# Twelve V loads cut by partitions, and a reordered turn, in an attention and MLP decode step with its gradients

## The chip, the cores and the metric

The kernel runs on one core of a Trainium2 chip. The metric is the device time of one execution in microseconds (us). A core has engines that run side by side: PE (matrix products; PEld is its weight load), DVE (vector operations), ACT (scalar functions and scaling), POOL and SP. In this kernel POOL only issues stores and SP only issues loads. The transfers themselves are done by 16 DMA engines, which all queues share. Each DMA engine that takes part in a transfer adds 1 to the transfer's semaphore when its part has landed, so that a transfer of 128 rows ends with 16 increments.

## The reference

One token x (1 x 640) goes through a block with attention over a cache of 8192 positions (32 heads of 192) and an MLP of width 1536, with layer norms modulated by a vector c. The function returns the output and, for a given grad_out, the gradients of nine inputs, those of the whole K and V cache among them. Cut to what fills the time:

```python
q = (x @ wq).reshape(B, Sq, Hq, Dh)                      # after layer norm and modulation
scores = einsum('bhqd,bhkd->bhqk', q, k) * Dh ** -0.5
p = softmax(scores)
o = einsum('bhqk,bhkd->bhqd', p, v);  ao = o @ wo
x1 = x + ga * ao                                         # then layer norms, MLP: gelu(n @ w3) @ w4
# gradients, per head: do is the gradient of o
# dV[k, :] = p[k] * do          dP[k] = sum_d V[k, d] * do[d]
# dS[k] = p[k] * (dP[k] - c)    dK[k, :] = dS[k] * q
```

K and V are 100.7 MB each, and so are dK and dV. V is read twice, once forward and once backward; K is read once.

## The kernel before, in words

**Layout.** The 8192 positions of a head lie as 64 rows on each of 128 partitions. Everything is done in halves: half t (0 or 1) of head h is a tile of 128 partitions x 32 rows x 192 values in bf16, that is 12288 bytes per partition and 1536 KB in all. In the diff "rows" of a load are partitions. `load_k` (L234) and `load_v` (L328) load such a half in one transfer, issued on SP.

**Forward (L592 to L659).** Step i of the loop works on three heads: it makes the scores of head i, scales K of head i-1 by its softmax weights, and ends the sums of head i-2. Scores: DVE multiplies a K half by q (`fwd_mult`, "prod" at L132), PE sums the products over d by matrix products with an identity (L372), DVE reduces them (L376), and after a maximum (L383 to L391) ACT takes the exponential (L393). ACT (L407) and DVE (L414) scale K rows by the weights into EK, and PE forms the products of V with EK (L432, L443, L449), from which both the forward output and, later, the gradient of q are made. In each second step a small sum (`fwd_tot`, L476) waits on PE until DVE has added up the part of ao (`fwd_ao_add`, L618), and DVE does that behind its second prod of the step. Loads are issued on SP in program order, per step V half 0, in each second step a wo tile (`fwd_wo`, L460), K half 1 of the next head, V half 1, K half 0 of the head after. Each waits for its buffer: three for V, five "big" ones for K.

**Turn (L660 to L1230).** After the last head comes a chain of small operations: the end of ao, two layer norms (`ln_cols`), w3 and a gelu, then back (du, dn2, two `ln_bwd_cols` named lb2 and lb1) to the gradient of ao, from which the first do is made (L1201 to L1207). Beside this chain, other work is put where an engine would wait: `dg_some(n)` does n of the 12 products d_g = w4 rows with dbo on DVE (0.82 us each, L546); `w3T_pe` and `w3T_act` transpose w3 on PE (L699) through PSUM banks and copy it out on ACT (L704); `woT_some(n)` transposes n of four groups of a wo tile in the same way (L712, L713). The argument `fill` of the layer norms says what is put into which wait. The first dV store is issued at the end of the turn, at 570.9 us.

**Backward (L1231 on).** Heads run from 31 down. Per head DVE and ACT make the two dV halves (L983, L1005), DVE multiplies the loaded V halves by do (`bwd_mult`, "V_sb" at L132), PE sums them to dP (L1000), DVE makes dS and the two dK halves (L983). POOL issues the stores of dV (L1008), dK (L1035) and of the smaller gradients. V halves come through a ring of six buffers (`ring_load`, L749), which now and then also takes a wo tile (`load_wo`); SP loads the next one when the buffer's last use is over. The stores' tiles come from the five big buffers.

The order of work on PE, DVE and ACT is that of the program (`pin_order`, L53). Loads on SP use eight semaphores in turn, so a load also waits until the load eight places ahead of it has landed.

Of the kernel before, what the change touches and what calls it, by code (L numbers as in the profile page):

```python
# [20 lines left out]
def kernel(  # L21
# [26 lines left out]
    nc = tc.nc  # L48
# [16 lines left out]
    P = 128  # L65
# [6 lines left out]
    JH = J // 2  # L72
# [10 lines left out]
    NP2 = DH // 2  # L83
    NA = 8
    NAV = 40
    assert S % P == 0 and D % P == 0 and QD % P == 0 and F % P == 0 and DH == 192

    const = ctx.enter_context(tc.tile_pool(name="const", bufs=1))
# [5 lines left out]
    def bank(tag, bufs=1, name=None, n=512):  # L94
        return psum[0].tile([P, n], FP32, tag=tag, name=name or "ps_" + tag, bufs=bufs)
# [32 lines left out]
    def ccol(n, name, dtype=FP32):  # L128
        return const.tile([P, n], dtype, name=name)

    def mul(out, a, b):
        nc.vector.tensor_tensor(out=out, in0=a, in1=b, op=ALU.mult)  # L132

    def add(out, a, b):
        nc.vector.tensor_tensor(out=out, in0=a, in1=b, op=ALU.add)
# [4 lines left out]
    def stt(out, in0, scalar, in1, op0, op1):  # L140
        nc.vector.scalar_tensor_tensor(out=out, in0=in0, scalar=scalar, in1=in1, op0=op0, op1=op1)  # L141
# [6 lines left out]
    def neg_means(parts, n, name):  # L148
        ps = bank_c(name)
        nc.tensor.matmul(ps[:, 0:n], lhsT=negd_mat, rhs=parts, start=True, stop=True)  # L150
        return ps[:, 0:n]
# [21 lines left out]
    def ln_bwd_cols(dn, n, rstd, add_to, out, pfx, fill=lambda: None):  # L173
        s = ccol(2, pfx + "_s")
        nc.vector.reduce_sum(out=s[:, 0:1], in_=dn, axis=AX.X)
        jk = ccol(NDC, pfx + "_jk")
        nc.vector.tensor_tensor_reduce(out=jk, in0=dn, in1=n, scale=1.0, scalar=0.0, op0=ALU.mult, op1=ALU.add, accum_out=s[:, 1:2])
        m_ps = neg_means(s, 2, pfx + "_m")
        fill()
        t = ccol(NDC, pfx + "_t")  # L180
        mul(t, n, m_ps[:, 1:2].to_broadcast([P, NDC]))
        add(t, t, dn)
        add(t, t, m_ps[:, 0:1].to_broadcast([P, NDC]))
        stt(out, t, rstd[:, 0:1], add_to, ALU.mult, ALU.add)
# [23 lines left out]
    V_hd = [A_v_cache[0, h].rearrange("(p j) d -> p j d", p=P) for h in range(HQ)]  # L208
# [25 lines left out]
    def load_k(h, t):  # L234
        tl = big_tile("K_sb")
        nc.sync.dma_start(out=tl, in_=K_hd[h][:, t * JH : (t + 1) * JH, :])
        return tl
# [30 lines left out]
    x0_c, c_c, dy_c = xcg[:, 0:NDC], xcg[:, NDC : 2 * NDC], xcg[:, 2 * NDC : 3 * NDC]  # L268
# [56 lines left out]
            return (0, P), (P, DH), 0, 3 * (h // 2), 3 * (h // 2) + 1  # L325
        return (DH - P, DH), (0, DH - P), DH - P, 3 * (h // 2) + 2, 3 * (h // 2) + 1

    def load_v(pool, h, t, slot):  # L328
        tl = pool.tile([P, JH, DH], BF16, name="V_sb", tag=f"v{slot}")
        nc.sync.dma_start(out=tl, in_=V_hd[h][:, t * JH : (t + 1) * JH, :])  # L330
        return tl

    def load_fwd(h, t, kind):
        if not 0 <= h < HQ:
            return
        if kind == "v":
            st[h]["V"].append(load_v(fv, h, t, (2 * h + t) % 3))
        elif (h, t) not in K_st:
            K_st[h, t] = load_k(h, t)

# [181 lines left out]
    def fwd_ao_add(hp, sm, c1=408):  # L522
        if hp == 0:
            dve_copy(ao_c, sm[:, c1 : c1 + NDC])
        else:
            add(ao_c, ao_c, sm[:, c1 : c1 + NDC])
# [4 lines left out]
    def w3n(i, lo, hi):  # L531
        return w_t[1][:, i * F + lo : i * F + hi] if i < 4 else w_t[0][:, lo:hi]

    def w4n(f, lo, hi):
        return w_t[0][:, F + f * D + lo : F + f * D + hi] if f < 7 else w_t[2][:, (f - 7) * D + lo : (f - 7) * D + hi]
# [3 lines left out]
    def dg_some(n):  # L539
        f0 = dg_next[0]  # L540
        f1 = min(f0 + n, NFC)
        dg_next[0] = f1
        for f in range(f0, f1):
            j0 = 5 * D + 12 * P + f % 2 * D
            jk = w_t[2][:, j0 : j0 + D]
            nc.vector.tensor_tensor_reduce(out=jk, in0=w4n(f, 0, D), in1=dbo_bc, scale=1.0, scalar=0.0, op0=ALU.mult, op1=ALU.add, accum_out=d_g[:, f : f + 1])  # L546

    st = {h: {"V": [], "prod": []} for h in range(HQ)}
# [21 lines left out]
    fv = ctx.enter_context(tc.tile_pool(name="fv", bufs=1, side="right", reuse_waits="tile"))  # L570
# [21 lines left out]
    for i in range(1, HQ):  # L592
        c, p, pp = 2 <= i < HQ, 0 <= i - 1 < HQ, 0 <= i - 2 < HQ
        n = i + 1 < HQ
# [84 lines left out]
    def w3T(blk, n=1):  # L679
        if blk < NB3:  # L680
            return w3T_t[:, blk * P : (blk + n) * P]
        c0 = 5 * D + (blk - NB3) * P
        return w_t[2][:, c0 : c0 + n * P]

    w3T_next = [0, 0]
    w3T_ps = {}
    NG3 = NFC * NDC // 4

    def w3T_pe(n):
        for g in range(w3T_next[0], min(w3T_next[0] + n, NG3)):  # L690
            b = g % 6
            if b in (0, 2):
                w3T_ps[g] = bank("s", 2, "t_ps", SB[0])
                w3T_ps[g + 1] = w3T_ps[g][:, 512:1024]
            elif b > 3:
                w3T_ps[g] = bank("ab"[b - 4], name="t_ps")
            for k in range(4):
                f, i = divmod(4 * g + k, NDC)
                nc.tensor.matmul(w3T_ps[g][:, k * P : (k + 1) * P], lhsT=w3n(i, f * P, (f + 1) * P), rhs=ident_bf, start=True, stop=True)  # L699
        w3T_next[0] += n  # L700

    def w3T_act(n):
        for g in range(w3T_next[1], min(w3T_next[1] + n, NG3)):
            nc.scalar.copy(out=w3T(4 * g, 4), in_=w3T_ps[g][:, 0:512])  # L704
        w3T_next[1] += n

    def woT_some(n):
        for g in range(woT_next[0], min(woT_next[0] + n, 4)):
            t_ps = bank("s", 2, "t_ps", SB[0])
            blks = range(4 * g, min(4 * g + 4, 3 * NDC))  # L710
            for k, blk in enumerate(blks):
                nc.tensor.matmul(t_ps[:, k * P : (k + 1) * P], lhsT=woT[:, blk * P : (blk + 1) * P], rhs=ident_bf, start=True, stop=True)  # L712
            nc.scalar.copy(out=woT[:, 512 * g : 512 * g + P * len(blks)], in_=t_ps[:, 0 : P * len(blks)])  # L713
        woT_next[0] += n
# [4 lines left out]
    fwd_kvK(hl - 1, 3, st[hl - 1])  # L719
    nc.scalar.copy(out=kb_sb, in_=kb_ps[:, 0 : 2 * DH])  # L720
    fwd_ao_add(HH - 2, sl_["sm"])
    dg_some(1)
    fwd_ao_add(HH - 1, sl_["sm"], 420)
    fek_cm.__exit__(None, None, None)
    fsm_cm.__exit__(None, None, None)
# [7 lines left out]
    HS = list(range(HQ - 1, -1, -1))  # L733
    PS = list(range(HH - 1, -1, -1))
    V_b = {HS[0]: st[HS[0]]["V"], HS[1]: {1: st[HS[1]]["V"][1]}}
# [10 lines left out]
    def ring_slot(n):  # L746
        return (3, 4, 5, 2, 0, 1)[n % NR]

    def ring_load():  # L749
        while ring_n[0] < len(ring) and (ring_n[0] < 3 or ring_key(ring_n[0] - NR) in freed):  # L750
            kind, k, t = ring[ring_n[0]]
            slot = ring_slot(ring_n[0])
            pool = bv if slot > 2 else fv
            ring_n[0] += 1
            if kind == "v":
                V_b.setdefault(k, {})[t] = load_v(pool, k, t, slot)
            else:
                load_wo(k, pool.tile([P, JH, DH], BF16, name="V_sb", tag=f"v{slot}"))

    def load_wo(k, tl):  # L760
        lo, n = PS[BATCHES[k][-1]], len(BATCHES[k])
        tl = tl.rearrange("p j d -> p (j d)")[:, 0 : 3 * n * D].rearrange("p (c r) -> p c r", r=D)
        nc.sync.dma_start(out=tl, in_=wo_v[:, 3 * lo : 3 * (lo + n), :])
        for hp in range(lo, lo + n):
            for cc in range(3):
                wo_src[hp, cc] = tl[:, 3 * (hp - lo) + cc, :]

    def ring_key(n):
        return ring[n] if n >= 0 else (("v", HS[0], 0), ("v", HS[0], 1), ("v", HS[1], 1))[n]
# [9 lines left out]
    def bwd_pf_act(h):  # L779
        bst[h]["PF"] = bsm.tile([P, J], FP32, name="PF")  # L780
        nc.scalar.activation(out=bst[h]["PF"], in_=E_all[:, h, :], func=ACT.Copy, scale=rinv_bc[:, h : h + 1])
# [7 lines left out]
        bwd_pf_dve(h)  # L789

    def ln1_fill(k):
        if k == 0:
            dg_some(1)
        else:
            w3T_pe(4)
            w3T_act(4)

    def ln2_fill(k):
        w3T_pe(1 + 2 * k)
        dg_some(1)  # L800

    x1_c = ccol(NDC, "x1_c")
    mul(x1_c, ao_c, ga)
# [1 line left out]
    n1_c, r1 = ln_cols(x1_c, "ln1", ln1_fill)  # L805
# [48 lines left out]
    for f in range(NFC):  # L854
        for i in range(NDC):
            nc.tensor.matmul(dn2_ps[:, i : i + 1], lhsT=w3T(f * NDC + i), rhs=du_bf[:, f : f + 1], start=False, stop=(f == NFC - 1), skip_group_check=True)
    bwd_pf_act(HS[0])
    dn2 = ccol(NDC, "dn2")
    dve_copy(dn2, dn2_ps[:, 0:NDC])
    mid_ps = {"h2": aux_ps[:, 32 : 32 + NDC]}  # L860
# [4 lines left out]
                nc.tensor.matmul(mid_ps["h2"][:, r : r + 1], lhsT=w4n(f, r * P, (r + 1) * P), rhs=g_bf[:, f : f + 1], start=False, stop=(f == 6), skip_group_check=True)  # L865

    def lb2_fill():
        woT_some(4)

    dhb = ccol(NDC, "dhb")  # L870
    ln_bwd_cols(dn2, n2_c, r2, dbo_c, dhb, "lb2", lb2_fill)
    dn1 = ccol(NDC, "dn1")
    mul(dn1, dhb, cb1)
    dx1 = ccol(NDC, "dx1")
    ln_bwd_cols(dn1, n1_c, r1, dy_c, dx1, "lb1")
    dao_bf = ccol(NDC, "dao_bf", BF16)
    mul(dao_bf, dx1, ga)
    bwd_pf_dve(HS[0])
# [123 lines left out]

    def bwd_dv_act(o, h, t, lo=0, hi=NAV // 2):
        for jj in range(lo, hi):
# [4 lines left out]

    def bwd_dv_dve(o, h, t, na=NAV // 2, ends=(JH,)):  # L1010
        j0 = t * JH
# [219 lines left out]
    for i in range(HQ):  # L1231
        h, nxt = HS[i], HS[i + 1] if i + 1 < HQ else None
# [48 lines left out]
        if i == I_SIDE:  # L1281
# [5 lines left out]
            for n in range(len(ring) - NR, len(ring)):  # L1287
                slot = ring_slot(n)
# [33 lines left out]
```

## Time and profile before

| what | value |
|---|---|
| time, median of 3 runs (lowest to highest) | 1380.68 us (1379.69 to 1381.73) |
| profiled execution, its own time | 1382.5 us |
| its span, from the first to the last instruction | 1380.7 us |
| busy share of the span: PE, DVE, ACT, POOL | 62%, 78%, 68%, 8% |
| read from and written to HBM | 341.51 MB, 225.91 MB |
| V half: transfers, KB, median from issue to landing | 125, 1536 KB, 14.2 us |
| K half | 64, 1536 KB, 14.4 us |
| dK half, store | 64, 1536 KB, 23.0 us |
| dV half, store | 61, 1536 KB, 22.4 us |
| ACT before dV products (L1005), waiting for dK stores | 60.6 us |
| DVE before dK products (L983), waiting for dK stores | 54.0 us |

The page divides the span into 40 equal slices of 34.5 us; the forward takes the first 15 or so, the turn two, the backward the rest. A digit in the slices is a busy share in tenths. Lines of a timeline give start, duration, engine, line, operation, tiles and, in brackets, how long the engine was idle before and what ended that. Lines of windows give the stretch, its length, the busy time and count of instructions of PE, PEld, DVE, ACT and POOL, then the granted PE clock (1.00 is full), the share of the 16 DMA engines' time that was busy, and GB/s. The trace also holds the start, length, queue and size of each DMA packet and the time of each semaphore increment; it does not say which DMA engine made them.

### The profile page before, as it was taken

What the parts mean: (1) busy time and instruction counts of PE and PEld (TensorE: products, weight loads), DVE (VectorE), ACT (ScalarE), POOL (GpSimd) and SP (SyncE); (2) the same over time, 40 slices, a digit from 0 to 9 for tenths busy, and PEclk for the clock granted to TensorE, in tenths of its full rate; (3) what the DMA queues carried; (4) which work ended last, traced back from release to release, by engine and by line L of the source; (5) the groups of instructions that cost most, each with busy time, mean ns of one, the idle gap of its engine ahead of it and who ended that gap; (6) DMA issues with size and microseconds to landing.
All of it is one profiled execution on the core that took longest, in us unless ns stands there. A gap on an engine that the chain in (4) does not pass through costs nothing. (4 is left out here: it accounts for less than half of the span.)

```text
span 1380.7 us, 28348 instructions
## 1 busy us (share of the span) xinstructions
PE 852.1 (62%) x11655; PEld 672.8 (49%) x11655; DVE 1070.6 (78%) x1273; ACT 945.0 (68%) x2586; POOL 112.0 (8%) x203
## 2 busy tenths in 40 slices
PE   3699999999999999738645744234332435324242
PEld 3577777777777777726534532123221323213131
DVE  3588778878887886799997977857757859579695
ACT  1388777877877884866786657576864866557781
POOL 0000000000000000111101101111111111021010
PEclk9799999999999998566666666666766666666665
DMA  9999999999999999899999999999999999999997
GB/s 392 416 415 420 419 418 420 421 411 418 418 419 407 418 417 376 311 381 422 409 425 427 427 426 428 428 426 427 420 423 421 407 427 426 429 423 406 429 428 311
DMA packets 73167, 569.25 MB, mean 412 GB/s; under 512 B 6862, under 2 KB 19918, under 8 KB 32846
## 3 DMA queue, kind: packets, MB, share of 16 engines
q1 hardware_dynamic: 48592, 341.52, 60.2%
q0 software_dynamic: 24416, 225.92, 38.9%
q8 instruction: 91, 1.49, 0.4%
q14 instruction: 38, 0.31, 0.1%
q10 hardware_dynamic: 30, 0.00, 0.0%
HBM read 341.51 MB, written 225.91 MB: 411 GB/s over the span
## 5 line engine op out<-in xcount | busy, mean ns | idle before, releaser
L1005 ACT ACTIVATE dV<-do_pb,PF 128x192 bf16<-128x192 bf16 x1246 | 434.6, 440 | 108.7 <-DMA out_dram<-dK 60.6
L1000 PE MATMUL dP_ps<-V_sb,ident_bf 128*128 128x256 bf16 (+1 forms) x1584 | 229.2, 319 | 246.8 <-DVE V_sb L132 246.8
L407 ACT ACTIVATE EK<-K_sb,E_f 128x192 bf16<-128x192 bf16 x992 | 351.1, 442 | 4.1 <-PE kb_ps L302 2.8
L1000 PEld LDWEIGHTS <-ident_bf 128*128 128x128 bf16 x1584 | 179.3, 116 | 296.3 <-issue 169.1
L983 DVE TENSOR_TENSOR dK<-dS,q_pb 128x6144 bf16<-128x6144 bf16 x64 | 213.2, 3354 | 59.4 <-DMA out_dram<-dK 54.0
L132 DVE TENSOR_TENSOR prod<-K_sb,q_pb 128x6144 bf16<-128x6144 bf16 x64 | 214.4, 3349 | 3.6 <-DMA K_sb<-in_A_k_cache_dram 3.6
L132 DVE TENSOR_TENSOR V_sb<-V_sb,do_pb 128x6144 bf16<-128x6144 bf16 (+1 forms) x66 | 212.0, 3253 | 0.0
L432 PE MATMUL ps_a<-EK,V_sb 128*128 128x193 bf16 x1984 | 192.9, 249 | 1.9 <-DMA V_sb<-in_A_v_cache_dram 1.9
L432 PEld LDWEIGHTS <-V_sb 128*128 128x128 bf16 x1984 | 165.6, 99 | 19.5 <-issue 12.7
L983 DVE TENSOR_TENSOR dV<-P2h,do_pb 128x2304 bf16<-128x2304 bf16 (+2 forms) x67 | 88.8, 1353 | 50.1 <-DMA out_dram<-dV 40.4
L414 DVE TENSOR_TENSOR EK<-K_sb,P2h 128x1536 bf16<-128x1536 bf16 x124 | 117.5, 949 | 0.0
L1008 POOL DMA_DIRECT2D out_dram<-dV x68 | 37.0, 545 | 934.9 <-DVE dV L983 607.7
L443 PE MATMUL ps_b<-EK,V_sb 128*64 128x193 bf16 x1984 | 109.3, 253 | 0.0
L372 PE MATMUL S_ps<-prod,ident_bf 64*64 64x256 bf16 x3072 | 101.7, 280 | 11.9 <-DVE prod L132 11.9
L372 PEld LDWEIGHTS <-ident_bf 64*64 64x64 bf16 x3072 | 86.7, 111 | 32.6 <-issue 28.3
L443 PEld LDWEIGHTS <-V_sb 128*64 128x64 bf16 x1984 | 81.9, 110 | 19.7 <-issue 16.1
L393 ACT ACTIVATE E_f<-sm_ps,negm 128x64 f32<-128x64 f32 x31 | 9.7, 314 | 104.4 <-DVE negm L391 104.4
L376 DVE TENSOR_REDUCE S<-S_ps 128x128 f32<-128x1024 f32 x32 | 39.2, 1224 | 49.0 <-PE S_ps L372 49.0
L449 PE MATMUL kb_ps<-EK,hot_bf 128*32 128x384 bf16 x992 | 64.8, 339 | 0.0
L1050 ACT ACTIVATE wq_o<-wq_bc,ha_f 128x1536 bf16<-128x1536 bf16 x12 | 18.4, 1564 | 44.4 <-DMA out_dram<-wq_o 44.4
L191 PE MATMUL bc_ps<-ident_bf,dq_bf 128*128 128x128 bf16 x48 | 6.4, 304 | 66.6 <-ACT do_pb L195 65.5
L1035 POOL DMA_DIRECT2D out_dram<-dK x64 | 35.3, 552 | 136.7 <-DVE dK L983 95.1
(266 smaller groups left out, 805.8 us busy)
## 6 DMA issues: line engine op xcount, KB each, us to landing
V_sb<-in_A_v_cache_dram SPq DMA_DIRECT2D x125, 1536.0 KB, 14.2
K_sb<-in_A_k_cache_dram SPq DMA_DIRECT2D x64, 1536.0 KB, 14.4
out_dram<-dK POOLq DMA_DIRECT2D x64, 1536.0 KB, 23.0
out_dram<-dV POOLq DMA_DIRECT2D x61, 1536.0 KB, 22.4
wq<-in_A_wq_dram SPq DMA_DIRECT2D x3, 2560.0 KB, 33.9
wo_t<-in_A_wo_dram SPq DMA_DIRECT2D x16, 480.0 KB, 14.9
out_dram<-dwo POOLq DMA_DIRECT2D x16, 480.0 KB, 18.2
wq<-in_A_wq_dram SPq DMA_DIRECT2D x4, 1920.0 KB, 28.3
```

What stands on the lines that cost most here:

```text
L132: nc.vector.tensor_tensor(out=out, in0=a, in1=b, op=ALU.mult)
L372: nc.tensor.matmul(st["S_ps"][c0 : c0 + 64, r, t * JH : (t + 1) * JH, :], lhsT=ident_bf[64 * r : 64 * r + 64, 64 * r : 64 * r + 64], rhs=p ...
L376: nc.vector.reduce_sum(out=st["S2"], in_=st["S_ps"], axis=AX.X)
L407: nc.scalar.activation(out=st["EK"][q][:, jj, 0:DH], in_=K_st[h, t][:, r * JQ + jj, :], func=ACT.Copy, scale=st["E_f"][:, j : j + 1])
L414: nc.vector.tensor_tensor(out=EK[:, NA:JQ, 0:DH].rearrange("p j (d r) -> p j d r", r=2), in0=K_st[h, t][:, r * JQ + NA : (r + 1) * JQ, :]. ...
L432: nc.tensor.matmul(st["A_ps"][:, 0:n], lhsT=V_sb[:, r * JQ + jj, a0:a1], rhs=EK[:, jj, 0:n], start=(q == 0 and jj == 0), stop=(q == 3 and ...
L443: nc.tensor.matmul(st["B_ps"][g : g + 64, 0:n], lhsT=V_sb[:, r * JQ + jj, b0:b1], rhs=EK[:, jj, 0:n], start=(q == 0 and jj < 2), stop=(q = ...
L449: nc.tensor.matmul(kb_ps[g : g + 32, 0 : 2 * DH], lhsT=hot_bf[:, HQ - 1 - h : 2 * HQ - 1 - h], rhs=EK[:, jj : jj + 2, 0:DH], start=(h == 0 ...
L983: nc.vector.tensor_tensor(out=o.rearrange("p j (d r) -> p j d r", r=2), in0=pairs[:, :, None, :].to_broadcast([P, n, NP2, 2]), in1=vec.rea ...
L1000: nc.tensor.matmul(bst[h]["dP_ps"][:, t * JH + r : t * JH + r + n, :], lhsT=ident_bf, rhs=V_sb[:, :, k * DS : (k + 1) * DS], start=(k == 0 ...
L1005: nc.scalar.activation(out=o[:, jj, :], in_=vec_of(do_pb, h), func=ACT.Copy, scale=bst[h]["PF"][:, t * JH + jj : t * JH + jj + 1])
L1008: st2.dma_start(out=dV_hd[h][:, t * JH + r0 : t * JH + r1, :], in_=o[:, r0:r1, :])
```

## The change

In the forward, half 1 of V of heads 6, 12, 18 and 24 is loaded in five transfers, of 8, 8, 8, 8 and 96 partitions, in place of one of 128. In the backward, half 1 of V of each fourth head (the third, the seventh and so on of 32: eight halves) is loaded in two, of 120 and 8 partitions. The bytes are the same. SP issues 16 and 8 more transfers; the other queues issue what they did.

In the turn, the d_g product between the two last sums of ao is taken out, and the waits of the layer norms get other numbers of d_g products: ln1 one and one (before one and none), ln2 none and one (before one and one). Ten of twelve are done ahead of du in place of eleven. The groups of w3's transpose start with banks a and b in place of the two s banks. Of wo's four transpose groups, one now stands ahead of lb2, two within it and one within lb1, in place of all four within lb2. On PE, DVE and ACT nothing else moves, and no instruction is added but that du is written in parts of 10 and 2 columns for 11 and 1.

```diff
+    CUT_F = (8, 8, 8, 8, 96)
+    CUT_B = (120, 8)
...
-    def load_v(pool, h, t, slot):
+    def load_v(pool, h, t, slot, cuts=(P,)):
         tl = pool.tile([P, JH, DH], BF16, name="V_sb", tag=f"v{slot}")
-        nc.sync.dma_start(out=tl, in_=V_hd[h][:, t * JH : (t + 1) * JH, :])
+        p0 = 0
+        for n in cuts:
+            nc.sync.dma_start(out=tl[p0 : p0 + n], in_=V_hd[h][p0 : p0 + n, t * JH : (t + 1) * JH, :])
+            p0 += n
         return tl
...
-            st[h]["V"].append(load_v(fv, h, t, (2 * h + t) % 3))
+            st[h]["V"].append(load_v(fv, h, t, (2 * h + t) % 3, CUT_F if t == 1 and h in (6, 12, 18, 24) else (P,)))
...
     def w3T_pe(n):
...
             b = g % 6
-            if b in (0, 2):
+            if b in (2, 4):
                 w3T_ps[g] = bank("s", 2, "t_ps", SB[0])
                 w3T_ps[g + 1] = w3T_ps[g][:, 512:1024]
-            elif b > 3:
-                w3T_ps[g] = bank("ab"[b - 4], name="t_ps")
+            elif b < 2:
+                w3T_ps[g] = bank("ab"[b], name="t_ps")
...
     fwd_ao_add(HH - 2, sl_["sm"])
-    dg_some(1)
     fwd_ao_add(HH - 1, sl_["sm"], 420)
...
-                V_b.setdefault(k, {})[t] = load_v(pool, k, t, slot)
+                V_b.setdefault(k, {})[t] = load_v(pool, k, t, slot, CUT_B if t == 1 and HS.index(k) % 4 == 2 else (P,))
...
     def ln1_fill(k):
-        if k == 0:
-            dg_some(1)
-        else:
+        dg_some(1)
+        if k == 1:
             w3T_pe(4)
             w3T_act(4)
 
     def ln2_fill(k):
         w3T_pe(1 + 2 * k)
-        dg_some(1)
+        dg_some(k)
...
     bwd_pf_act(HS[0])
+    woT_some(1)
...
     def lb2_fill():
-        woT_some(4)
+        woT_some(2)
+
+    def lb1_fill():
+        woT_some(1)
...
-    ln_bwd_cols(dn1, n1_c, r1, dy_c, dx1, "lb1")
+    ln_bwd_cols(dn1, n1_c, r1, dy_c, dx1, "lb1", lb1_fill)
```

## Prediction

> **What bounds the kernel now.** I read the page's slices first, then the queues, the windows of single stretches, the waits, and at last the trace's records of packets and semaphore increments.
>
> ```profile
> DMA  9999999999999999899999999999999999999997
> GB/s 392 416 415 420 419 418 420 421 411 418 418 419 407 418 417 376 311 381 422 409 425 427 427 426 428 428 426 427 420 423 421 407 427 426 429 423 406 429 428 311
> q1 hardware_dynamic: 48592, 341.52, 60.2%
> q0 software_dynamic: 24416, 225.92, 38.9%
> q8 instruction: 91, 1.49, 0.4%
> ```
>
> The 16 DMA engines are busy from end to end at 410 to 429 GB/s; no compute engine is over 78%. So the DMA engines set the time, and what can be won is only where some of the sixteen are out of work while others are not. Two windows show that state (the columns end with granted clock, DMA share and GB/s):
>
> ```profile
> 535.40:536.40 1.00, 1.00 (x30) 0.59 (x29) 1.00 (x3) 1.00 (x4) 0.00 (x0) 1.00 0.57 225
> 1364.00:1371.00 7.00, 0.00 (x0) 0.00 (x0) 0.57 (x1) 0.00 (x0) 0.54 (x1) 0.50 1.01 421
> 1372.00:1378.00 6.00, 0.00 (x0) 0.00 (x0) 0.00 (x0) 0.00 (x0) 0.00 (x0) 0.50 0.06 27
> ```
>
> A share of 0.06 is one engine of sixteen: from 1372 us on, a single one works off its part of the last stores. At 535 us about half of them work. The increments say the same. Each transfer adds 16, one per engine. Those of the last store lie between 1371.3 and 1372.8 us, but for one at 1379.2. That gap to the 15th was 0.3 us near 825 us, 2.1 near 968, 5.0 near 1046 and 6 from 1310 on: **one engine falls behind in the backward**. In the forward it is **eight**: of the load that landed at 298.7 us, eight increments came within the first 2.9 us and eight between 5.6 and 7.5. Instruction fetches do that: the packet records have 72 fetches of 16 KB (queue q8) by 561 us, one in 7.2 us; after the first, at 14.3 us, the last increment's gap goes from 0.07 to 1.55 us, and each later one delays another engine by some 1.5 us, in turn over eight. 72/8 x 1.5 = 13.5 us for each of the eight.
>
> What the lag costs the forward is seen by pairs of heads, between issues of every second wo load:
>
> ```profile
> 99.72:130.86 31.14, 29.75 (x548) 23.55 (x545) 25.96 (x40) 24.79 (x74) 0.00 (x0) 1.00 1.01 419
> 161.98:193.38 31.40, 29.75 (x548) 23.55 (x545) 26.04 (x40) 24.78 (x74) 0.00 (x0) 1.00 1.01 418
> 193.38:226.31 32.93, 31.25 (x548) 24.40 (x545) 26.05 (x40) 24.80 (x74) 0.00 (x0) 0.95 1.01 419
> 288.57:321.54 32.97, 31.25 (x548) 24.34 (x545) 26.04 (x40) 24.79 (x74) 0.00 (x0) 0.95 1.00 409
> 415.06:448.13 33.07, 31.24 (x548) 24.38 (x545) 26.02 (x40) 24.78 (x74) 0.00 (x0) 0.95 1.00 408
> ```
>
> Undisturbed pairs take 31.14 us at clock 1.00; three take 1.8 to 1.9 more at 0.95. Their cause, in order of time:
>
> ```profile
> 136.77 0.38 PE L476 MATMUL sm_ps<-rowsum,ones_mat_f 128*128 128x2 f32 x2 [1.07 <-DVE ao_c L135]
> 168.17 0.38 PE L476 MATMUL sm_ps<-rowsum,ones_mat_f 128*128 128x2 f32 x2 [1.33 <-DVE ao_c L135]
> 196.11 3.36 DVE L132 TENSOR_TENSOR prod<-K_sb,q_pb 128x6144 bf16<-128x6144 bf16 x1 [0.20 <-DMA K_sb<-in_A_k_cache_dram]
> 199.59 0.38 PE L476 MATMUL sm_ps<-rowsum,ones_mat_f 128*128 128x2 f32 x2 [1.36 <-DVE ao_c L135]
> ```
>
> PE always waits 1.07 us there. A K half late by 0.20 us makes it 1.36, and the clock dips; late by 0.17 (at 164.7) gave 1.33 and no dip. The K halves at 291, 418 and 513 us are late by 0.24, 0.36 and 0.53, with dips. So four dips of some 1.85 us, and 0.3 of smaller delay: 7.7 us in all.
>
> **The change part by part.** A V half has 128 rows of 12288 bytes; the packet records give 0.46 us for one. A transfer of 128 rows has 16 increments, 8 rows each; the 5-row loads at the start (queue q10) had five data packets and five increments each. From these two rows I take that n rows go to the largest number of engines up to 16 that shares them evenly, always from the same first one: 8 rows to the first eight, 96 to sixteen (6 each), 120 to fifteen (8 each). The Trainium skill, "DMA: Bandwidth & Descriptors", section "Why a DMA increments its semaphore by 16 and not by 1", states just this, with the lowest-numbered engines used; no run here shows it for 8, 96 or 120.
>
> Which engines are fetched on? I followed the packets of the five engines of the 5-row loads: of the first five fetches at least four hit none of them. With eight engines in turn, the slow eight then can't be the first eight. So each forward split gives the slow eight 6 rows for 8 and the others 10.
>
> *Forward (heads 6, 12, 18, 24).* 2 x 0.46 = 0.92 us less for the slow eight per split, 3.7 in all. How fast do they lose ground? After the dip at 196 us compute stood 1.85 us back, yet at 291, three pairs on, a K half was late by 0.24: 2.1 us in three pairs; from 291 to 418 it was 2.2 in four, from 418 to 513, 2.4 in three: 0.67 us per pair. With the splits (issued at 139 us, before the K half awaited at 165, and then every three pairs) I get slack +0.75 at 165, +0.08 at 196, -0.6 at 227 (a dip, +1.85), then +0.92 every third pair: next late near 415, none by 513. Two of four dips remain: **-3.9 us**; the ends are 0 and 7.7. What hides the extra rows of the fast eight: they lie 5 us ahead. What hides the four extra issues a split (0.33 us each on SP): SP has 3 to 7 us between issues, and transfers land 14.2 us after issue, so some four are queued.
>
> *Turn.* One d_g product leaves the place between the two ao_c sums, on the path: 549.23 to 549.97, so -0.66. One moves into the wait for ACT's square root (0.82 us where DVE idles 1.03), one behind du, where PE still has 50 of 60 products to do: both nothing; that cover gone, 0.8. One wo transpose group goes ahead of the lb2 sum, into PE's 0.53 us wait (4 products, half of 1.01), and one behind the lb1 sum, which started at 566.34 for its inputs' 565.8: -0.4. The swap of PSUM banks in w3T only changes which ACT copy is awaited; nothing, 0.3 either way. **-1.1**; ends 0 and -1.3. DMA is the bound again from 572 us on, so this goes to the end.
>
> *Backward (eight halves in 120 and 8).* The sixteenth engine loses 8 x 8 x 0.46 = 29.4 us of work; the first eight gain 8 x 0.46 = 3.7. The slow one is behind by 6.4 and has held others up: slices at 1080, 1240 and 1260 us moved 397, 407 and 409 GB/s for 428, 3.3 us lost, where ACT and DVE wait for stores (60.6 and 54.0 us over the backward). If the slow one is the sixteenth, it stops being last, and the end is where the other fifteen are: -6.5. Against it the first eight's 3.7, of which I take half (fetches after 583 us, 18 of them, cost the other eight 18/8 x 1.5 = 3.4, so the first eight have room); for it half of the 3.3. **-6.4**; ends -2.8 and -9.8. The halves aren't awaited: DVE's V_sb products idle 0.0 us.
>
> Sum: 3.9 + 1.1 + 6.4 = 11.4. The profiled execution (1382.5, its span 1380.7 and 1.8 around it) becomes 1371.1; the median of the runs, 1.8 lower, goes from 1380.7 to **1369.3**. All good ends: 18.8, so 1361.9; all bad: 2.8, so 1377.9.
>
> **Rivals.**
> 1. *The slow engine is among the first eight.* No record names it. Then it gets 3.7 more and the tail grows: -3.9 - 1.1 + 3.7 = -1.3, 1379.4. The Trainium skill, same page, section "Latency and other measured facts", calls engines 7 and 15 usually slower; by that it could be either, though the trace has one. 9%.
> 2. *Slower: 120 rows run on eight engines, 15 each* (a power of two). The first eight get 15 + 1 rows for 8: 8 x 8 x 0.46 = +29.4 at the end, with the turn and forward -5.0 and the tail -6.5: 1398.6. It decides from three rows more per half for the busiest engine (11.4 / 8 / 0.46). For it: no odd count stands in the trace. Against: five rows went to five. 5%.
> 3. *SP holds loads back.* Five pieces use five of eight semaphores; the second K half after a split waits for the K half before it. If the queues ran dry for a transfer, 4 x 3.7 = 14.8: +3.4, 1384.1. Against: three halves, 11 us, are queued then. 5%.
> 4. *Splitting moves nothing between engines.* The skill, same page, section "Rules for kernel authors", says of two transfers to disjoint partition halves not to bother, since they share the same engines. Then only the turn is won: 1379.6. Against: shares of 0.57 and 0.06. 4%.
>
> **How the numbers follow.** Forecast 77%, rivals as above. From no change a measurement of this kernel tells about 0.2%, 2.8 us. Faster: the forecast and a bit, 78%. Same: rivals 1 and 4 but for that bit, 12%. Slower: rivals 2 and 3, 10%. The range takes the bounds of the unknown costs, 1362 to 1378; what lies outside is 2 and 3, half of 1 and 4, and misses of the bounds.
>
> **What would show it.** Forward: pairs of heads at 31.1 us, clock 0.95 in two or fewer. Turn: first dV store some 5 us earlier than 570.9. Backward: the last store's increments within 4 us, no window with a share of 0.06. Wrong if a half's increments spread more than before (rivals 1, 2), or if DVE idles before prod for K right behind a split (3).

## The result, and the profile after

The change makes the kernel slower: 1434.26 us median (four runs, 1431.98 to 1436.74) against 1381.2 before (four runs, one more than in the table above), a ratio of 1.037 (1.031 to 1.042). The profiled execution has a span of 1431.4 us, 50.7 more than before. Its page:

```profile
DMA  9999999999999999999999999999999999999997
GB/s 390 415 418 417 329 419 398 332 403 388 339 402 365 367 389 403 311 366 384 416 402 424 424 402 427 417 425 426 403 427 426 407 424 426 413 423 403 414 412 331
q1 hardware_dynamic: 48776, 341.52, 61.4%
q0 software_dynamic: 24416, 225.92, 37.8%
q8 instruction: 91, 1.49, 0.4%
```

The DMA engines are as busy as before, from end to end, with the same bytes. But the shares are of a longer span: queue q1 (the loads) kept the engines for 61.4% of 1431.4 = 878.9 us, where it was 60.2% of 1380.7 = 831.2. So **the same loads took 47.7 us more of every engine's time**, and the stores 4.0 more (541.1 for 537.1). That is the whole loss. The engines were no more idle than before; the packets themselves took longer.

The dents in GB/s say where: slices 5, 8, 11 and 13 to 14 are the four forward cuts. The windows between wo loads, the four with a cut and two without, and among them the 14 us behind the first cut (the columns end with granted clock, DMA share and GB/s):

```profile
100.43:133.15 32.72, 31.33 (x548) 24.83 (x545) 25.96 (x40) 24.79 (x74) 0.00 (x0) 0.95 1.01 419
133.15:170.92 37.77, 32.69 (x552) 25.33 (x552) 26.59 (x44) 25.35 (x76) 0.00 (x0) 0.91 1.01 333
146.00:160.00 14.00, 11.52 (x214) 9.06 (x217) 11.86 (x19) 12.43 (x37) 0.00 (x0) 1.00 1.00 203
203.61:234.75 31.14, 29.76 (x548) 23.55 (x545) 25.96 (x40) 24.79 (x74) 0.00 (x0) 1.00 1.01 419
234.75:277.20 42.45, 33.04 (x548) 25.88 (x545) 26.28 (x41) 24.94 (x75) 0.00 (x0) 0.88 1.01 332
340.88:382.92 42.04, 32.13 (x552) 25.14 (x552) 26.30 (x42) 25.04 (x75) 0.00 (x0) 0.92 1.00 338
446.80:486.75 39.95, 31.85 (x548) 24.83 (x545) 26.04 (x40) 24.79 (x74) 0.00 (x0) 0.91 1.01 340
```

The third line is the finding: share 1.00 and 203 GB/s. The kernel before moved 425 GB/s in the same 14 us, at the same share:

```profile
146.00:160.00 14.00, 13.84 (x259) 10.94 (x259) 12.53 (x22) 11.94 (x36) 0.00 (x0) 1.00 1.01 425
```

In the packet records a row of 12288 bytes takes 0.46 us up to 145 us, from 146 to 160 us 0.77 to 1.65, and 0.46 again from 161 us on. No packet of 0.46 stands between, so all engines were slow. In the 14 us 2.8 MB were moved, about two halves: not the cut half alone was slow, but a whole load beside it too. The first dV store stands for the end of the turn (start, length, engine, line), here after and before:

```profile
612.45 0.69 POOL L1015 DMA_DIRECT2D out_dram<-dV  x1 [610.79 <-DVE dV L990]
570.93 0.68 POOL L1008 DMA_DIRECT2D out_dram<-dV  x1 [569.28 <-DVE dV L983]
```

So 41.5 us of the 50.7 arise up to there, and 9.2 in the backward. (Up to there lie the four forward cuts and the first of the backward, which is loaded ahead of the first store.)

The increments show how the pieces ran. A transfer on fewer than 16 engines adds the missing number at its issue: the 120 partitions have one early update and 15 others, the 8 have one early and 8 others. So the rows did go to fifteen and to eight engines, as predicted. The Trainium skill, "DMA: Bandwidth & Descriptors", section "Why a DMA increments its semaphore by 16 and not by 1", states this, and the trace agrees. In one pair of pieces seven of the 8 landed between 727.45 and 729.34 us and one at 739.79: there one of the eight engines that take 8 rows was itself far behind.

### The profile page after: what moved, and what is told of

It is laid out like the page before. It is cut to its first block, busy times and chain, and to the rows that moved or that the text cites. A ratio compares the mean times of both kernels' runs of the same rounds, so it can differ in the third digit from the quotient of the medians.

```text
span 1431.4 us, 28409 instructions
## 1 busy us (share of the span) xinstructions
PE 867.4 (61%) x11655; PEld 683.4 (48%) x11655; DVE 1071.6 (75%) x1273; ACT 945.9 (66%) x2586; POOL 112.1 (8%) x203
## 3 DMA queue, kind: packets, MB, share of 16 engines
q1 hardware_dynamic: 48776, 341.52, 61.4%
## 5 line engine op out<-in xcount | busy, mean ns | idle before, releaser
L1007 PEld LDWEIGHTS <-ident_bf 128*128 128x128 bf16 x1584 | 180.0, 117 | 309.4 <-issue 181.1
L437 PE MATMUL ps_a<-EK,V_sb 128*128 128x193 bf16 x1984 | 200.4, 255 | 14.0 <-DMA V_sb<-in_A_v_cache_dram 12.6
L437 PEld LDWEIGHTS <-V_sb 128*128 128x128 bf16 x1984 | 171.6, 101 | 33.2 <-issue 26.0
L1015 POOL DMA_DIRECT2D out_dram<-dV x68 | 36.9, 543 | 984.1 <-DVE dV L990 642.8
L1118 PEld LDWEIGHTS <-ident_bf 128*128 128x128 bf16 x112 | 13.8, 124 | 66.7 <-issue 62.8
## 6 DMA issues: line engine op xcount, KB each, us to landing
out_dram<-dwo POOLq DMA_DIRECT2D x16, 480.0 KB, 17.9
```

Of the source, the lines that this page charges most:

```text
L437: nc.tensor.matmul(st["A_ps"][:, 0:n], lhsT=V_sb[:, r * JQ + jj, a0:a1], rhs=EK[:, jj, 0:n], start=(q == 0 and jj == 0), stop=(q == 3 and ...
L1007: nc.tensor.matmul(bst[h]["dP_ps"][:, t * JH + r : t * JH + r + n, :], lhsT=ident_bf, rhs=V_sb[:, :, k * DS : (k + 1) * DS], start=(k == 0 ...
L1015: st2.dma_start(out=dV_hd[h][:, t * JH + r0 : t * JH + r1, :], in_=o[:, r0:r1, :])
```

## Experiments

The kernels e_turn, e_front and e_back take parts of the change away. The four probes compute nothing of the reference and only move data, so that a packet can be seen by itself; their figures are from the packet records.

### The parts alone

In e_turn both cuts are taken out of the change, as below. e_front takes out only CUT_B and so keeps the forward cut; e_back takes out only CUT_F.

```diff
-    CUT_F = (8, 8, 8, 8, 96)
-    CUT_B = (120, 8)
+    CUT_F = (128,)
+    CUT_B = (128,)
```

> The change without any cut: the reordered turn alone. By the two traces the turn got about 1.2 us shorter (first dV store to the end of the forward), so 1380.0 us, within 1378.5 to 1381.5, whichever theory of the cuts holds. If the turn were part of the loss, 1385 or more.

Measured: 1381.81 us, ratio 1.0003 (0.9991 to 1.0014): no change that can be told. From the last wo load to the first dV store it took 33.72 us (536.13 to 569.85), before 34.95 (535.98 to 570.93). So the turn did become 1.2 us shorter, but the interval at the end reaches from 1.2 less to 1.9 more; whether the gain gets there stays open.

> The change with the four forward cuts and the turn, and no backward cut. Port theory and all others that put the loss where the traces show it: first dV store near 612 us as in the changed kernel (570.9 before), and the 42 us carry to the end, since the backward is full of transfers: 1423 us, within 1417 to 1428. If the backward gives some of it back, below 1415. If the loss is made by both cuts together, below 1400.

Measured: 1422.37 us, 1.0303 (1.0286 to 1.0319); first dV store at 609.86. Over e_turn that is 40.6 us, **10.1 per forward cut**.

> The change with the eight backward cuts and the turn, and no forward cut. The traces put some 9 us between the first dV store and the end on the backward: 1381.2 - 1.2 + 9.2 = 1389 us, within 1385 to 1393. Port theory: 120 and 8 rows share groups for a few us per cut, about 1.2 us each. The prediction's engine counting alone (one engine relieved) would give 1374 to 1378.

Measured: 1392.98 us, 1.0083 (1.0068 to 1.0098), at the upper edge. Over e_turn 11.2 us, **1.4 per backward cut**. And 40.6 + 11.2 = 51.8 of the change's 52.5 over e_turn: the cuts add up. The slow engine of the tail is still there: of the last store 15 increments came by 1384.60 us, one at 1389.98.

### What makes a packet slow

The first probe loads V rows in twelve shapes, every load alone. In its list the first slice is of partitions, the second of rows in HBM; c makes both the same:

```diff
...
+        ("half", [c(0, 64)]),
+        ("even", [c(0, 128, 2)]),
+        ("near", [c(0, 8)]),
+        ("spread", [c(0, 32, 4)]),
+        ("nearfar", [(slice(0, 8), slice(0, 32, 4))]),
+        ("spreadnear", [(slice(0, 32, 4), slice(0, 8))]),
...
+            for dst, src in pieces:
+                nc.sync.dma_start(out=tl[dst], in_=V_hd[k % 32][src, (k // 32) * JH : (k // 32 + 1) * JH, :])
```

> This kernel computes nothing of the reference: it loads V rows of 12288 bytes in twelve shapes, four times each, every load alone, and stores one small row. Port theory: the 128 partitions fall into 16 groups of eight (0-3 with 32-35, 4-7 with 36-39, and so on to 28-31 with 60-63; the same above 64), a group takes one row in 0.46 us, and rows that several engines bring to one group at once share that. Then: full (128 rows) 0.46 us per packet; near (8 rows to partitions 0-7, two groups) about 4 x 0.46 = 1.85 us per packet; spread (8 rows to partitions 0, 4 .. 28, eight groups) 0.46; nearfar (rows to 0-7 from memory rows 0, 4 .. 28) 1.85 as near; spreadnear 0.46 as spread; sixteen (16 rows, eight groups) 0.92; half (64 rows, eight groups) as long in all as full, packets 0.92; even (64 rows, all groups) between 0.46 and 0.92; upper (96 rows) and most (120 rows) no sooner done than full, with packets above 0.46 where two engines meet. Rival, memory theory: the slow packets come from which rows of HBM are read together. Then nearfar is as quick as spread, and spreadnear as slow as near. Rival, piece theory: each piece costs a fixed time of its own and its rows run at 0.46 us whatever the partitions; then near and spread are alike, 0.46 per packet, and upper and most are done sooner than full.

SP's issues in it (each line: start, time from the first issue to the last of four; a load is issued when the one before has landed, so a third of it is one load):

```profile
59.47 22.30 SPq L82 DMA_DIRECT2D upper<-in_A_v_cache_dram  x4
88.68 29.26 SPq L82 DMA_DIRECT2D most<-in_A_v_cache_dram  x4
127.06 19.80 SPq L82 DMA_DIRECT2D half<-in_A_v_cache_dram  x4
152.72 14.60 SPq L82 DMA_DIRECT2D even<-in_A_v_cache_dram  x4
171.51 10.41 SPq L82 DMA_DIRECT2D near<-in_A_v_cache_dram  x4
184.98 9.34 SPq L82 DMA_DIRECT2D spread<-in_A_v_cache_dram  x4
196.59 10.27 SPq L82 DMA_DIRECT2D nearfar<-in_A_v_cache_dram  x4
209.98 9.06 SPq L82 DMA_DIRECT2D spreadnear<-in_A_v_cache_dram  x4
```

| shape, alone | median of a packet | first packet's start to last one's end |
|---|---|---|
| full, 128 rows | 0.46 us | 5.0 us (8 x 0.46 = 3.7, but 14 to 18 packets took over 0.7) |
| most, 120 rows | 0.90 to 0.95 | 7.8 |
| upper, 96 rows | 0.78 to 0.81 | 5.6 |
| half, 64 rows to 0-63 | 0.90 to 0.94 | 4.1 |
| even, 64 rows to 0, 2 .. 126 | 0.46 | 2.9 |
| the five pieces of the forward cut | 0.90 to 0.93 | 10.1 |
| the two pieces of the backward cut | 0.92 to 0.94 | 8.7 |

120 rows take longer than 128, and 64 neighbours twice a packet's time though nothing else runs; 64 partitions over the whole range do not. The piece theory falls (even is as much a piece as half). The 8-row loads agree with the group rule in sign at best: near and nearfar landed 0.35 to 0.4 us later than spread and spreadnear whatever the rows of HBM, where four rows on a group should have cost 1.4, and the packets themselves don't differ (medians of 0.5 to 0.8 us in all four). Why a lone burst shows so little is open. Of the 128 packets of the five pieces, 47 to 50 took over 1.2 us. The second probe adds two whole K halves behind each cut:

```diff
+            nc.sync.dma_start(out=ta, in_=K_hd[h][:, t * JH : (t + 1) * JH, :])
+            nc.sync.dma_start(out=tb, in_=K_hd[h + 1 if h < 31 else 0][:, t * JH : (t + 1) * JH, :])
```

> Again a kernel that computes nothing of the reference: it loads one V half in a given cut, with two whole K halves queued behind it, and waits for all three before the next; four times for each cut. The last three probes load 64 rows alone. Reckoned with the group rule as the first probe left it (two engines on a group: 0.92 us a row for both; 8 rows per engine in order), in us of transfers: full 3 x 3.7 = 11.0; cutfive (8, 8, 8, 8, 96) 20.0, for the engines come out of step and go on meeting in the loads behind; cuttwo (120, 8) 17.0; halves (0-63, then 64-127) 14.7; evens (partitions 0, 2 .. 126, then the odd ones) 11.0; spreadfive (8 rows to partitions 0, 4 .. 28 and so on, then 96) 14.5; near (32 rows as four times 8 neighbours) longer than spread (the same 32 rows as four times 8 rows four apart). If the loads behind do not suffer, cutfive is only 5 us over full, as it was alone. Of the 64 rows alone: the group rule goes by the destination, so halfeven (to 0-63, from even rows) takes 0.92 us a packet as half did, and evenhalf (to even partitions, from rows 0-63) 0.46 as even did; memory theory the other way round.

Measured from the first packet to the last: full 12.2 us; **cutfive 18.5 to 19.8**; cuttwo 17.2 to 17.6; **halves 15.4; evens 12.3 to 12.9**; spreadfive 16.1 to 17.5 (above the 14.5 reckoned); near 13.2 to 13.4, spread 11.4 to 12.7. The 64 rows alone: halfeven 0.93 to 0.95 us a packet as half, evenhalf 0.46 as even. So the destination decides, and the memory theory falls. The loads behind suffer too: cutfive is 6.7 over full here, 5.1 alone.

What the runs show, then: a row takes 0.46 us in a transfer to all 128 partitions or to every second one, and 0.8 to 0.95 us in one to 64, 96 or 120 neighbours; for the 64 it made no difference which rows of HBM they came from. The reading that fits is that two engines then write to one group of partitions and share what it takes in. The Trainium skill, "SBUF — State Buffer", section "Door 1: The DMA port swizzle (why `[64,N]` ≈ `[32,N]`)", gives these groups as ports of some 27 GB/s, and says that partitions 0 to 63 reach only eight. The trace agrees: 12288 bytes in 0.46 us are 26.7 GB/s, and half ran at 64 x 12288 bytes in 4.1 us = 192 GB/s. Which engine brought which row is not recorded; that two met is inferred from the doubled time, and which partitions make up a group isn't shown by these runs.

### The same in the kernel

```diff
-        p0 = 0
-        for n in cuts:
-            nc.sync.dma_start(out=tl[p0 : p0 + n], ...)
+        for c in cuts:
+            nc.sync.dma_start(out=tl[c], in_=V_hd[h][c, ...])
```

The cuts are now slices of partitions. e_halves: CUT_F is 0:64 and 64:128. e_evens: CUT_F and CUT_B are 0:128:2 and 1:128:2. e_spread: CUT_F is 0:32:4, 1:32:4, 2:32:4, 3:32:4 and 32:128. Where CUT_B isn't named the backward is uncut.

> The change with the four forward halves cut into two transfers of 64 neighbouring partitions (0-63, 64-127), no backward cut, the turn as changed. Group theory: 64 neighbours lie in eight groups, each brought by two engines, so a half takes 7.4 us of transfers for 3.7: four times 3.7 later, 1381.8 + 14.7 = 1396 us, within 1390 to 1404. Piece theory (only pieces on fewer than 16 engines, or the unequal ones, cost): each engine has 4 + 4 rows as before, so 1382, as in evens.

Measured: 1411.52 us, 1.02 (1.0175 to 1.0226). Slower by 29.7 over e_turn, 7.4 per cut: the sign of the group theory, twice its size.

> The change with all twelve halves, forward and backward, cut into two transfers of 64 partitions, the even ones and the odd ones; the turn as changed. As many rows per transfer, engines and issues as halves, but each transfer lies in all 16 groups. Group theory: no loss, 1381.8 us, within 1379 to 1385. Piece theory (a fixed cost for each cut): as halves per forward cut, so 1396 or more.

Measured: 1381.58 us, 0.999 (0.9975 to 1.0004): **twelve cuts, and no loss**. The same 14 us as above, e_halves first, then e_evens:

```profile
146.00:160.00 14.00, 11.54 (x221) 9.05 (x219) 11.43 (x19) 11.72 (x34) 0.00 (x0) 1.00 1.00 235
```

```profile
146.00:160.00 14.00, 13.84 (x259) 10.88 (x258) 12.53 (x22) 11.94 (x36) 0.00 (x0) 1.00 1.00 420
```

Two transfers of 64 partitions in both, the same rows per transfer and the same issues: 235 GB/s or 420.

> The change with the forward cuts of 8, 8, 8, 8 and 96, but the four pieces of 8 are partitions 0, 4 .. 28; 1, 5 .. 29; and so on, so that each lies in eight groups and not in two; no backward cut, the turn as changed. Same engines, rows, pieces and issues as the forward cut of the change (1422.4). Group theory: the pieces of 8 run at full speed, the 96 (eight groups with twice the rows of the others) still costs: some 3.5 us per cut in place of 10, so 1396 us, within 1388 to 1406. If only the number or the size of the pieces counts: 1422, as there.

Measured: 1409.98 us, 1.0183 (1.0155 to 1.0212). Spreading the pieces of 8 saves 12.4 us of e_front's 40.6, so nearness counts here too; the other 28.2, 7.0 per cut, go with the 96 and with what the cut does to its neighbours. That is again twice what I had reckoned.

### Why a cut costs more in the kernel than alone, and more in the forward

> Computes nothing of the reference: a whole K half, then one V half in a cut, then three whole K halves, all queued at once, four times for each cut; then the same with the first eight engines put out of step by three pieces of 8 rows of 24576 bytes ahead (partitions four apart). Open is why a cut costs more in the kernel (cutfive 10, halves 7.4 us) than in the second probe (6.7 and 3.2 us over full). Theory step: an engine that is behind or ahead writes to a group while its owner works on another load, so each cut also slows the load ahead and those behind it, the more the engines are out of step. Then laghalves over lagfull is near 7, lagcutfive over lagfull near 10, while halves over full without lag stays near 3. Theory depth: a whole load ahead is enough, and halves over full is near 7 without lag too. If both differences stay near 3 and 6.7, what the kernel adds is not made by the order of the transfers alone.

```diff
+            for j in range(3 if lag else 0):
+                r = slice(j, 4 * lag, 4)
+                nc.sync.dma_start(out=lg[r], in_=V_hd[h][r])
+            nc.sync.dma_start(out=pre, in_=K_hd[h][:, 0:JH, :])
...
```

With a lag (lag is 8) three loads of 8 rows go ahead, so that eight engines start late. From the first packet of 12288 bytes to the last, means of four rounds (three for the uncut one in step); the rows put ahead, of 24576 bytes, start 1.8 us earlier and are not counted:

| over the same with an uncut half | engines in step | first eight behind |
|---|---|---|
| uncut, itself | 19.8 us | 22.4 us |
| halves | +3.6 | **+10.2** |
| cutfive | +6.5 | +6.8 |
| cuttwo | +5.4 | +7.5 |

Whole loads do not mind being out of step: of their 640 packets 9 to 14 took over 0.7 us, in step 18 to 20. A cut does: halves costs almost three times as much (its rounds took 31.3 to 34.8 us, the uncut ones 22.0 to 22.9), where I had expected near 7. The kernel's engines are out of step as well (the prediction's load at 298.7 us landed over 7.5 us), and its 7.4 lies between 3.6 and 10.2, so it is accounted for in kind. For cutfive, expected near 10, this lag changed nothing, and its 10.1 in the kernel for 6.5 here stays open; another pattern of lag wasn't tried.

In e_front2 the forward gets the backward's cut:

```diff
-    CUT_F = (8, 8, 8, 8, 96)
+    CUT_F = (slice(0, 120), slice(120, 128))
```

> The change with the four forward halves cut as the backward ones are (120 and 8), no backward cut, the turn as changed. Open is why a backward cut costs only 1.45 us (1393.0 - 1381.4, over eight) and a forward one 10. Place theory: in the backward two thirds of the transfers are stores, so engines seldom meet in a group; the shape 120 and 8 itself costs 5.2 us in the second probe, and in the forward, with the ratio that cutfive and halves show (10 / 6.7, 7.4 / 3.2), 8 to 12: four times that over 1381.8, 1413 to 1430 us. Shape theory: 120 and 8 is simply the milder cut, so four times 1.45 to 5.2: 1388 to 1403.

Measured: 1418.38 us, 1.0257 (1.0228 to 1.0286): 36.6 over e_turn, **9.1 per cut of 120 and 8 in the forward, for 1.4 in the backward**. The shape isn't mild; the place is.

> Computes nothing of the reference: a whole K half, one V half in a cut, two whole K halves, as in the third probe without lag, and beside them four stores of 1536 KB queued at the same time; what is stored is one tile of no meaning. Open is why a cut of 120 and 8 costs 9.1 us in the forward and 1.45 in the backward. Place theory: stores take turns with the loads on each engine, so two engines seldom write to one group at the same moment: cuttwo over full falls from 5.4 us (third probe, loads alone) to below 2.5, cutfive from 6.4 to below 4, halves from 3.6 to below 2. If the differences stay, it is not the mixing with stores that makes the backward mild.

```diff
+            for j in range(4):
+                nc.gpsimd.dma_start(out=O_hd[2 * k + j // 2][:, (j % 2) * JH : (j % 2 + 1) * JH, :], in_=ts)
```

POOL's first issue of stores in two successive rounds each, for uncut, halves, cutfive and cuttwo; the difference within a pair is one round:

```profile
112.98 2.10 POOL L86 DMA_DIRECT2D out_dram<-ts  x4 [31.44 <-DVE ta L77]
146.12 2.10 POOL L86 DMA_DIRECT2D out_dram<-ts  x4 [31.04 <-DVE ta L77]
216.78 2.10 POOL L86 DMA_DIRECT2D out_dram<-ts  x4 [33.10 <-DVE ta L77]
252.31 2.10 POOL L86 DMA_DIRECT2D out_dram<-ts  x4 [33.42 <-DVE ta L77]
359.92 2.10 POOL L86 DMA_DIRECT2D out_dram<-ts  x4 [33.99 <-DVE ta L77]
396.33 2.10 POOL L86 DMA_DIRECT2D out_dram<-ts  x4 [34.31 <-DVE ta L77]
505.22 2.10 POOL L86 DMA_DIRECT2D out_dram<-ts  x4 [34.03 <-DVE ta L77]
541.83 2.10 POOL L86 DMA_DIRECT2D out_dram<-ts  x4 [34.51 <-DVE ta L77]
```

A round takes 33.1 us uncut and 35.5, 36.4 and 36.6 with a cut. By the packet records, which leave out the landing, halves costs 1.9 us over uncut, cutfive 2.8 and cuttwo 2.75 (expected: below 2, 4 and 2.5). So with stores beside the loads a cut costs about half (2.75 for cuttwo, where the second probe, with as many loads behind the cut, had 5.1). The backward's 1.4 has two stores for each load, and this probe one; what that second store does wasn't measured.

## Why the prediction was wrong

**The step that failed is the price of a row**: "the packet records give 0.46 us for one", used for rows of 8, 96 and 120 alike. That figure is the time of a row in a transfer of 128. I treated it as the engine's, to be moved from a slow engine to a fast one. The runs show that it depends on where the row lands beside what the other engines write. In the cut shapes a row takes 0.8 to 1.5 us, and slows rows of the whole loads near it. The spread of rows over engines, which I had held for the uncertain step, was right.

In the kernel this term can be added up: for each packet of 12288 bytes the time above 0.462 us, summed and divided by 16 engines. The last two rows, each taken over the kernel before, set it beside the spans of the same profiled executions:

| us | before | changed | e_turn | e_front | e_front2 | e_halves | e_spread | e_evens | e_back |
|---|---|---|---|---|---|---|---|---|---|
| 100 to 620 us | 11.9 | 50.3 | 11.9 | 45.3 | 42.8 | 39.0 | 34.9 | 11.1 | 15.4 |
| from 620 us | 6.9 | 17.6 | 5.4 | 10.8 | 11.5 | 9.8 | 10.0 | 7.8 | 16.2 |
| both, over before | | 49.1 | -1.5 | 37.3 | 35.5 | 30.0 | 26.1 | 0.1 | 12.8 |
| span, over before | | 50.7 | -3.8 | 39.1 | 36.9 | 28.2 | 29.1 | -1.4 | 10.8 |

The slow packets come to 49.1 of the 50.7 us, and in all eight kernels the two last rows agree within 3 us. In e_back the first cut, issued at about 546 us when no store runs yet, adds 3.5 to the upper row; the other seven add 9.3 to the lower, 1.3 each.

- *Forward, -3.9.* It came out as +40.6. The hidden gain can't be seen beside this. e_evens, which is not meant to move rows between engines, still has three pairs of 33.3 to 33.5 us at clock 0.95, like the dips of before.
- *Turn, -1.1.* The trace has -1.2 up to the first store, one trace on each side, so that the closeness may be chance; at the end it is not resolved.
- *Backward, -6.4* (its terms, 6.5 less 1.85 and with 1.65 more, give 6.3). It came out as +11.2. The tail did not go: in e_back one engine ends 5.4 us behind the rest, 6.4 before, though the engine that the pieces of 120 leave out had 29.4 us of work less, by the price of 0.46. So in that run the slow one was among the fifteen; whether among the first eight, as rival 1 has it, no record shows. Rival 1's price, 1379.4, was small beside what came. I had also taken the lag for a fixed quantity, from one trace: on the last store it is 1.8 us in e_evens, 2.6 in e_front, 3.4 in the changed kernel and 5.0 in e_turn. And it is a lag of stores: before, the dK store issued at 1274.92 us had its last increment 11.4 us behind the 15th, while the V load issued at 1275.71 had all sixteen within 1.1 us.
- *Rival 2 (120 on eight engines).* No: fifteen increments. Its sign was right, its mechanism wrong.
- *Rival 3 (SP holds loads back).* Its sign came: from 100 to 560 us SP waited three times for a K half to land, 17.9 us in all (never before the change), and after the first cut, at 173 us, the prod product idled 0.56 us for its K half. But the DMA share is 1.00 through the slow stretch, so the queues never ran dry, and the holding back isn't what cost the time.
- *Rival 4.* I took the advice against splitting of the Trainium skill, "DMA: Bandwidth & Descriptors", section "Rules for kernel authors", as "moves nothing", and gave it 4%. Its other half, to use one transfer of 128 partitions, was the warning; I never asked what a shape of fewer partitions does to a packet. The runs agree for evens, where nothing was lost or won (ratio 0.999); for halves they show a cost, 7.4 us per cut, where the rule only says not to bother.

The shape of the error: of each piece I costed the issue, the count of rows and the semaphores, and kept the one price that the trace showed only for whole transfers. My bound for it was 0.46 on both sides. "Wrong if a half's increments spread more than before" named the sign, but under two rivals only.

## What to carry to other kernels

A packet's time belongs to the shape of its transfer and to what runs beside it, not to the engine alone: before cutting a load by partitions, ask which partitions the engines write at the same moment, and measure one such transfer alone. If a load must be cut, cut it so that each piece spans all partitions with a stride, as in evens. And when DMA share is 1.00, read GB/s beside it: busy engines moved half as much here.

## What the runs showed of the hardware that I had not expected

- Moving fewer rows took longer: 120 rows alone 7.8 us, 128 rows 5.0.
- Whole loads run at 0.46 us a packet also with eight engines held up by three extra rows each; once a cut is among them, packets of whole loads are slow too, for 15 to 20 us at each cut of this kernel's forward.
- Eight rows to eight neighbouring partitions landed only 0.35 to 0.4 us later than to eight spread ones, while in the five pieces, queued one behind another, more than a third of the packets took over 1.2 us. Why the lone eight are so quick is open.
